# Set-up of a convolution and maxout kernel: where x buffers are zeroed, idle matmuls beside the band, and the engine of some weight differences

## The chip, the cores and the metric

The kernel runs on one core of a Trainium2 chip. The metric is device time in microseconds of one execution. Times inside an execution come from a hardware profile of it, counted from the span's start. The engines are named as in the profile: PE is TensorE (PEld its weight loads), DVE VectorE, ACT ScalarE, POOL GpSimd, SP SyncE, which here only issues transfers (SPq is its queue).

## What is computed

A light convolution over time (7 taps, one softmaxed set of weights for each of 8 heads of 24 channels) is followed by a maxout layer and an output matrix. Shapes: x is 8 x 4160 x 192, so 33280 tokens; w1, w2, w3 are 192 x 768; w_out is 768 x 192.

```python
w = exp(weight - max); w = w / (sum(w) + 1e-09)          # 8 heads x 7 taps
y[b, s, h, g] = sum_k w[h, k] * x_pad[b, s + k, h, g]     # x_pad: 6 rows of zeros ahead
h = maximum(maximum(y @ w1, y @ w2), y @ w3)
out = h @ w_out
```

The kernel uses max(a, b, c) = c + max(0, a - c, b - c): it forms the differences w1 - w3 and w2 - w3 (`wd`), so that ScalarE's Relu gives max(0, a - c), VectorE takes the maximum with b - c, and the part of c goes through one matrix M = w3 @ w_out (`m16`).

## The kernel before

The 33280 tokens make 65 tiles of 512. A tile's stages are: load x as fp32, cast to fp16, convolve as matmuls with a band matrix (`band`, built from the 7 taps of each head), bring the result to channels by tokens, multiply by `wd` (`l1`), and multiply by w_out and M (`st2`). The first four tiles (0 to 3, "dense") are convolved from `xz` straight into channels by tokens; from tile 4 on the convolution's result goes through a DMA transpose (`turn`) and GpSimd makes a second copy of it for the other half of the partitions (`double`).

x buffers and their zeroing. There are seven buffers. Those of blocks 0 to 3 are used again by blocks 7 to 10, in another layout with more rows, some of which must be zero. `get_x` zeroes them on GpSimd when a block asks for its buffer:

```python
def get_x(t):
    if not 0 <= t < NB or t in xin:
        return
    if t < XBUF:                                     # XBUF = 7, NDENSE = 4
        xbuf.append(const.tile([P, NR, D], FP32, name=f"xf_{t}"))
    xf = xbuf[t % XBUF if t < NDENSE + XBUF else NDENSE + (t - NDENSE - XBUF) % 3]
    if NDENSE <= t < NDENSE + XBUF:
        nc.gpsimd.memset(xf[TOK:HALF, 0 if t < XBUF else NQ:NR, :], 0.0)
    xin[t] = [xf, 0, ()]
# load_x(t, eng=nc.sync) calls get_x(t), then issues the loads of the block
```

The beginning: the loads, the idle matmuls that keep TensorE at work, and the band (38 small matmuls into two PSUM tiles, which ScalarE and VectorE copy out):

```python
load_x(0); load_wa(...); load_x(1); load_wb(...); ...      # weights in pieces, then w_out
for t in range(2, 7):
    load_x(t)
...
keep_warm(6, psp, "p")                                     # 6 matmuls of 512 columns, result unused
nc.scalar.activation(out=wexp[:], in_=wk[:], func=AF.Exp, accum_out=wsum[:])
nc.vector.reciprocal(out=wrec[:], in_=wsum[:])
nc.vector.tensor_scalar_mul(out=line[:, 31:31 + KW], in0=wexp[:], scalar1=wrec[:])   # L259
for v in range(2):
    nc.vector.memset(xz[1][v][:], 0.0)
cast_dense(0, (nc.vector.tensor_copy, nc.vector.tensor_copy))                        # L200
CUT = 25
for lo, hi, copy in ((0, CUT, nc.scalar.copy), (CUT, WIN, nc.vector.tensor_copy)):
    for c in range(lo, hi):
        if c % 13 == 0:
            nc.tensor.matmul(beside[:], lhsT=idle[HALF:P, 0:P], rhs=idle[HALF:P, :], ...)  # L269
        nc.tensor.matmul(bps[:, c - lo, :], ...)                                     # L270
    for a in range(4):
        copy(out=band[32 * a:32 * a + 32, ...], in_=bps[:]...)                       # L273
keep_warm(2, psp, "p")
```

The weight differences, and the copies by which one of them reaches the other half of the partitions:

```python
def make_wd(n, j0, j1, eng=nc.vector):                                               # L287
    f = slice(P * j0, P * j1)
    eng.tensor_sub(out=wd[:, n, f], in0=ws[:, n, f], in1=w3s[:, n // 2, f])

def cross_wd():
    nc.vector.tensor_copy(out=wd[0:HALF, NC, :], in_=wd[HALF:P, 0, :])               # L299
    nc.scalar.copy(out=wd[HALF:P, NC, :], in_=wd[0:HALF, 1, :])
```

Where the later tiles meet the queues. In iteration t the loop issues, on the SyncE queue and in this order, the store of tile t - 2, loads, and the transposes of a tile convolved in it; `load_x(9)` comes in iteration 3 ahead of `turn(5)`, which brings tiles 5 and 6:

```python
if t in (3, 4):
    double(t + 1)                                          # GpSimd, L411
...
elif t == 3:
    cast_x(7); cast_x(8)                                   # GpSimd, L183
...
op(lambda t=t: (store(t - 2, 0, 4, (nc.sync,)), load_x(9) if t == 3 else None))
... # l1 and st2 of the iteration, on TensorE; conv(u) and its evictions (L388)
turn(u)                                                    # SyncE, L402
load_on(t)
```

Of the kernel before, what the change touches and what calls it, by code (L numbers as in the profile page):

```python
# [10 lines left out]
FP32 = mybir.dt.float32  # L11
# [4 lines left out]
P = 128  # L16
# [5 lines left out]
NBLK = 512  # L22
# [6 lines left out]
def kernel(  # L29
# [88 lines left out]
# [4 lines that stand above are left out]
        if t < XBUF:  # L122
            xbuf.append(const.tile([P, NR, D], FP32, name=f"xf_{t}"))
        xf = xbuf[t % XBUF if t < NDENSE + XBUF else NDENSE + (t - NDENSE - XBUF) % 3]
        if NDENSE <= t < NDENSE + XBUF:
            nc.gpsimd.memset(xf[TOK:HALF, 0 if t < XBUF else NQ:NR, :], 0.0)  # L126
        assert all(v[0] is not xf for v in xin.values())
        xin[t] = [xf, 0, ()]

    def load_x(t, eng=nc.sync):  # L130
        if not 0 <= t < NB:
            return
        loaded.add(t)
        get_x(t)
        xf = xin[t][0]
        if t < NDENSE:
            todo = [(0, c[3], c[1] * SEQ + c[2], i) for i, c in enumerate(chunks_of[t])]
        else:
            todo = [(HALF * (i // NR) + (0 if s else LAP), KR if s else TOK,
                     b * SEQ + s - (LAP if s else 0), i % NR) for i, (b, s) in enumerate(rows_of(t))]  # L140
        parts = []
        i, n = 0, len(todo)
        row = [c[2] for c in todo]
        while i < n:
            k = i
            while k + 1 < n and todo[k + 1][:2] == todo[i][:2] and row[k + 1] - row[k] == row[i + 1] - row[i]:
                k += 1
            step = row[i + 1] - row[i] if k > i else 0
            p0, rlen, _, q0 = todo[i]
            q1 = todo[k][3] + 1  # L150
            src = bass.AP(tensor=x.tensor, offset=row[i] * D,
                          ap=[[D, rlen], [step * D, q1 - q0], [1, D]])
            eng.dma_start(out=xf[p0:p0 + rlen, q0:q1, :], in_=src)
            if parts and parts[-1][0] == rlen:
                parts[-1] = (rlen, parts[-1][1], q1)
            else:
                parts.append((rlen, q0, q1))
            i = k + 1
        xin[t] = [xf, todo[0][0], parts]
# [31 lines left out]
    def cast_dense(t, copies):  # L191
        xf, _, parts = xin.pop(t)
        for v, copy in enumerate(copies):
            if copy is None:
                continue
            for s in range(CYC // 32):
                cut = GRP * (32 * s // GRP + 1)
                a, b = (32 * s, cut) if v == 0 else (cut, 32 * s + 32)
                for (rl, q0, q1) in parts:
                    copy(  # L200
                        out=xz[t][v][0:rl, q0:q1, :].rearrange("p q (k c) -> p q k c", c=CYC)[:, :, :, a:b],
                        in_=xf[0:rl, q0:q1, :].rearrange("p q (k c) -> p q k c", c=CYC)[:, :, :, a:b])
# [27 lines left out]
    make_identity(nc, ident[:])  # L230
    ident16 = const.tile([P, P], FP16)
    nc.gpsimd.tensor_copy(out=ident16[:], in_=ident[:])
    for t in range(2, 7):
        load_x(t)
    idle = const.tile([P, NBLK], FP16)
    nc.vector.memset(idle[:], 0.0)
    def keep_warm(n, pool=psw, tag="w"):

        ps = pool.tile([P, NBLK], FP32, tag=tag, name="idle")
        for _ in range(n):  # L240
            nc.tensor.matmul(ps[:], lhsT=idle[:, 0:P], rhs=idle[:], start=True, stop=True)  # L241
# [8 lines left out]
        nc.vector.memset(xz[0][v][:], 0.0)  # L250
    band = const.tile([P, NHEAD, BAND_W], FP16)
    nc.vector.memset(band[:], 0.0)
    keep_warm(6, psp, "p")
    wexp = const.tile([NHEAD, KW], FP32)
    wsum = const.tile([NHEAD, 1], FP32)
    nc.scalar.activation(out=wexp[:], in_=wk[:], func=AF.Exp, accum_out=wsum[:])  # L256
# [3 lines left out]
    for v in range(2):  # L260
        nc.vector.memset(xz[1][v][:], 0.0)
    cast_dense(0, (nc.vector.tensor_copy, nc.vector.tensor_copy))
    CUT = 25
    beside = psw.tile([P, NBLK], FP32, tag="w", name="beside")
    for lo, hi, copy in ((0, CUT, nc.scalar.copy), (CUT, WIN, nc.vector.tensor_copy)):
        bps = psq.tile([32, hi - lo, NHEAD], FP32, tag="q", name=f"band_{lo}")
        for c in range(lo, hi):
            if c % 13 == 0:
                nc.tensor.matmul(beside[:], lhsT=idle[HALF:P, 0:P], rhs=idle[HALF:P, :], start=True, stop=True)  # L269
            nc.tensor.matmul(bps[:, c - lo, :], lhsT=line[:, WIN - 1 - c:WIN + 31 - c],  # L270
                             rhs=ident16[0:NHEAD, 0:NHEAD], start=True, stop=True)
        for a in range(4):
            copy(out=band[32 * a:32 * a + 32, :, 32 * a + lo:32 * a + hi],  # L273
                 in_=bps[:].rearrange("p c h -> p h c"))
    keep_warm(2, psp, "p")

# [6 lines left out]
# [3 lines that stand above are left out]
# [5 lines left out]
    def cast_w3(j0, j1):  # L293
        f = slice(P * j0, P * j1)
        nc.gpsimd.tensor_copy(out=w3h[:, 0, f], in_=w3s[:, 0, f])
        nc.gpsimd.tensor_copy(out=w3h[0:HALF, 1, f], in_=w3s[0:HALF, 1, f])

    def cross_wd():
        nc.vector.tensor_copy(out=wd[0:HALF, NC, :], in_=wd[HALF:P, 0, :])  # L299
        nc.scalar.copy(out=wd[HALF:P, NC, :], in_=wd[0:HALF, 1, :])  # L300

    def side(i, c):
# [8 lines left out]
    def transpose_w3(g):  # L311
        ps = psw.tile([P, 2, D], FP32, tag="w", name=f"pt{g}")
        for k in range(2):
            js = slice(P * (2 * g + k), P * (2 * g + k + 1))
            for n in range(2):
                row = slice(0, HALF if n else P)
                nc.tensor.matmul(ps[:, k, P * n:min(P * (n + 1), D)], lhsT=w3h[row, n, js],  # L317
                                 rhs=ident16[row, row], start=True, stop=True)
        nc.scalar.copy(out=w3t[:, 2 * g:2 * g + 2, :], in_=ps[:])
# [39 lines left out]
    def conv_dense(t, copies):  # L359


        yd = dense[t] = ydp.tile([P, NC, NBLK], FP16, tag="yd", name=f"yd_{t}")
        for n, slots_ in enumerate(((0, 1, 2, 3), (4, 5, 4, 5))):
            ps = psw.tile([P, NBLK], FP32, tag="w", name=f"D{n}_{t}")
            for (q, b, row_lo, rlen, lo, hi, cc) in chunks_of[t]:
                for v in range(2):
                    for g, s in enumerate(slots_):
                        h = (32 * s + 31 * v) // GRP
                        nc.tensor.matmul(  # L369
                            ps[32 * g:32 * g + 32, lo:hi],  # L370
                            lhsT=xz[t][v][0:rlen, q, 32 * s:32 * s + 32],
                            rhs=band[0:rlen, h, cc:cc + hi - lo],
                            start=(v == 0), stop=(v == 1), tile_position=(0, 32 * g))
            copies[n](out=yd[:, 2 * n, :], in_=ps[:])  # L374
# [128 lines left out]
    def l1_dense(tiles):  # L503

        meet()
        ps = {}
        for t, j, pools in tiles:
            for i, (pool, tag) in enumerate(pools):
                ps[t, j, i] = pool.tile([P, NBLK], FP32, tag=tag, name=f"l{tag}{i}_{t}_{j}")
                nc.tensor.matmul(ps[t, j, i][:], lhsT=wd[:, i, P * j:P * (j + 1)], rhs=dense[t][:, 0, :],  # L510
                                 start=True, stop=False)
        for t, j, _ in tiles:
            for i in range(2):
                nc.tensor.matmul(ps[t, j, i][:], lhsT=w_of(i, NC - 1, j), rhs=y_all(t, i, NC - 1),  # L514
                                 start=False, stop=True)
        return [lambda t=t, j=j: top(t, j, (ps[t, j, 0], ps[t, j, 1])) for t, j, _ in tiles]
# [95 lines left out]
    make_wd(2, 0, 2)  # L612
    cast_dense(1, (nc.gpsimd.tensor_copy, ACT))
    a, b = l1_dense([(0, 0, PQ), (0, 1, PQ)])
    a()
    cast_w3(0, 2)
    conv_dense(1, (ACT, ACT))
    make_wd(0, 2, 4)
    make_wd(1, 2, 4)
    b()  # L620
    copy_w3(ACT, 2, 6)
# [2 lines left out]
    a()  # L624
    b()
    transpose_w3(0)
    make_wd(0, 4, 6)
    a, b = l1_dense([(0, 2, PQ), (0, 3, WW)])
    cast_w3(2, 6)
    a()  # L630
    make_wd(1, 4, 6)
    b()
    for f in l1_dense([(1, 2, PQ), (1, 3, WW)]):
        f()
    for f in l1_dense([(0, 4, PQ), (0, 5, WW)]):
        f()
    transpose_w3(1)
    transpose_w3(2)
    nc.gpsimd.tensor_copy(out=wo[:], in_=wos[:])
    cast_dense(2, (nc.gpsimd.tensor_copy, nc.gpsimd.tensor_copy))  # L640
    cast_dense(3, (nc.gpsimd.tensor_copy, nc.gpsimd.tensor_copy))
    cast_x(4)
    for f in l1_dense([(1, 4, PQ), (1, 5, WW)]):
        f()
    make_m(0)
    make_m(1)
    st2(0, (10, 10))
    meet()
    conv_dense(2, (ACT, DVE))
    cross_wd()  # L650
    cross(2)
    for u in range(2, NJ):
        st2(0, (5 * u + 5, 5 * u + 5))
# [104 lines left out]
```

## Time and profile before

| | |
|---|---|
| time, median of 3 runs | 461.1 us (460.49 to 464.15) |
| span of the profiled execution | 461.4 us |
| TensorE busy | 453.4 us, 98% |
| VectorE, ScalarE, GpSimd busy | 78%, 69%, 44% |
| idle matmuls L241, first 62 us | 9, 4.4 us busy |
| "beside" matmuls L269 | 3, 1.8 us busy |
| zeroing of x, GpSimd L126 | 7, 6.2 us busy |
| subtractions L287, VectorE | 8, 3.9 us busy |

A line of the profile names the line of the kernel (L126), the engine, the operation and the tiles, written tile first. In the timeline a row merges neighbours of one kind; its first two numbers are start and length in us, and the bracket says how long the engine had been idle and what ended that. A wait that is put down to one engine can be of several. PEclk is the share of its full clock that TensorE was granted; in the first 12 us, before its first record, it is shown as full although the matmuls there are slow.

### The profile page before, as it was taken

To read this page: it belongs to the slowest core of one execution; us is meant where nothing else is said; L and a number is where in the kernel's file an instruction comes from. 1 tells how busy PE (TensorE), PEld (TensorE's weight loads), DVE (VectorE), ACT (ScalarE), POOL (GpSimd) and SP (SyncE) were. 2 spreads that over 40 slices of the span, in tenths; PEclk is the share of its full clock that TensorE was granted. 3 is DMA by queue.
4 is the path that set the end of the run, shared out by engine and by line. 5 is a ranking of instruction groups with operands and counts; after the bars stand their busy time and mean duration, and the time that the engine had idled before them with its cause. 6 is when DMAs were issued, how large, how long until landed. Compare 5 with 4: busy or idle time off the path is not lost.

```text
span 461.4 us, 18767 instructions
## 1 busy us (share of the span) xinstructions
PE 453.4 (98%) x7832; PEld 414.2 (90%) x7832; DVE 359.4 (78%) x617; ACT 317.0 (69%) x605; POOL 204.2 (44%) x227
## 2 busy tenths in 40 slices
PE   8999799999999999999999999999999999999997
PEld 4368689999999999999999999999999999999996
DVE  7757667778878788787878888787887878787776
ACT  3757466667767677766766777676777767676664
POOL 5456455165744354434546454533645344504000
PEclk9999989999999999999999999999999999999999
DMA  7946986687794977959596885859686694525223
GB/s 196 214 83 164 180 172 176 181 192 186 185 209 126 168 163 173 187 120 191 138 182 146 168 199 131 178 133 189 161 180 161 144 182 134 132 72 108 68 70 104
DMA packets 127988, 72.04 MB, mean 156 GB/s; under 512 B 52064, under 2 KB 127711, under 8 KB 127903
## 3 DMA queue, kind: packets, MB, share of 16 engines
q1 hardware_dynamic: 127743, 70.75, 69.2%
q8 instruction: 61, 1.00, 1.0%
q14 instruction: 24, 0.20, 0.2%
q10 hardware_dynamic: 160, 0.10, 0.1%
HBM read 33.28 MB, written 25.56 MB: 128 GB/s over the span
## 4 chain that ended last, share of the span: by engine, by line
PE 96%; DVE 1%; issue 1%; DMA 1%; ACT 1%; POOL 0%; ACTq 0%; POOLq 0%; DVEq 0%
PE po L558 36%; PE lq L494 31%; PE lp L494 21%; PE G L350 3%; PE D L369 1%; DMA yp<-ys 1%; PE lw L510 0%; PE lq L510 0%; PE lp L514 0%; PE pt L317 0%; PE lp L510 0%; POOL yp L411 0%; PE idle L241 0%; PE band L270 0%; ACT L256 0%
## 5 line engine op out<-in xcount | busy, mean ns | idle before, releaser
L558 PE MATMUL po<-wo,h 64*128 64x192 f16 x3120 | 337.6, 243 | 0.2 <-DVE yd L374 0.2
L482 DVE TENSOR_TENSOR h<-r,lq 128x512 f16<-128x512 f16 x385 | 264.0, 686 | 92.4 <-ACT r L481 82.5
L481 ACT ACTIVATE r<-lp 128x512 f16<-128x512 f32 x385 | 229.9, 597 | 121.2 <-PE lp L494 106.4
L494 PE MATMUL lp<-yp,wd 64*128 64x512 f16 x1098 | 296.9, 377 | 1.7 <-POOL yp L411 1.7
L494 PE MATMUL lq<-yp,wd 64*128 64x512 f16 x1098 | 296.7, 377 | 0.9 <-POOL yp L411 0.9
L558 PEld LDWEIGHTS <-h 64*128 64x128 f16 x3120 | 246.4, 94 | 8.9 <-issue 5.7
L494 PEld LDWEIGHTS <-wd 64*128 64x128 f16 x2268 | 179.0, 94 | 13.4 <-issue 2.7
L183 POOL CAST x<-xf 103x768 f16<-103x768 f32 x122 | 97.3, 827 | 118.8 <-DMA xf<-in_x_dram 85.9
L558 PE MATMUL po<-m,yp 64*128 64x192 f16 x732 | 143.6, 244 | 0.0
L411 POOL COPY yp<-yp 64x1536 f16<-64x1536 f16 (+1 forms) x62 | 89.6, 1445 | 88.2 <-DMA yp<-ys 48.6
L567 DVE TENSOR_TENSOR o<-a,po 128x384 f32<-128x384 f32 (+1 forms) x132 | 71.4, 542 | 2.5 <-PE po L558 1.3
L558 PEld LDWEIGHTS <-yp 64*128 64x128 f16 x732 | 67.5, 94 | 0.7
L566 ACT COPY a<-po 128x384 f32<-128x384 f32 (+1 forms) x132 | 61.7, 468 | 1.9 <-PE po L558 1.5
L388 ACT CAST ys<-G 128x384 f16<-128x384 f32 x61 | 26.3, 482 | 10.7 <-PE G L350 10.7
L388 DVE CAST ys<-G 128x384 f16<-128x384 f32 x61 | 31.0, 550 | 0.0
L350 PE MATMUL G<-x,band 39*32 39x192 f16 (+2 forms) x1216 | 17.8, 231 | 0.0
L350 PEld LDWEIGHTS <-band 39*32 39x32 f16 x1216 | 11.3, 91 | 4.9 <-issue 4.7
L494 PE MATMUL lq<-yd,wd 64*128 64x512 f16 x36 | 9.9, 376 | 0.3 <-issue 0.3
L494 PE MATMUL lp<-yd,wd 64*128 64x512 f16 x36 | 9.9, 376 | 0.0
L558 PE MATMUL po<-m,yd 64*128 64x192 f16 x48 | 7.5, 243 | 0.0
L369 PEld LDWEIGHTS <-xz 112*32 112x32 f16 x320 | 4.6, 108 | 2.5 <-issue 1.7
L126 POOL MEMSET xf<- 32x576 f32 (+1 forms) x7 | 6.2, 916 | 0.2
(61 smaller groups left out, 86.3 us busy)
## 6 DMA issues: line engine op xcount, KB each, us to landing
xf<-in_x_dram SPq DMA_DIRECT2D x113, 234.0 KB
out_dram<-o SPq DMA_DIRECT2D x62, 384.0 KB
xf<-in_x_dram SPq DMA_DIRECT2D x7, 204.8 KB
xf<-in_x_dram SPq DMA_DIRECT2D x3, 420.0 KB
ws<-in_moe_w_dram SPq DMA_DIRECT2D x8, 128.0 KB
yp<-ys SPq DMA_TRANSPOSE x62
out_dram<-o SPq DMA_DIRECT2D x5, 192.0 KB
wos<-in_moe_w_out_dram SPq DMA_DIRECT2D x1, 576.0 KB
```

What stands on the lines that cost most here:

```text
L126: nc.gpsimd.memset(xf[TOK:HALF, 0 if t < XBUF else NQ:NR, :], 0.0)
L183: nc.gpsimd.tensor_copy(out=x16s[t0][0:K, :, :, u, r, :].rearrange("p h j c -> p j h c"), in_=xf[0:K, 4 * r:4 * r + 4, :].rearrange("p j ( ...
L350: nc.tensor.matmul(G[2 * (k // per) + i][TOK * j:TOK * (j + 1), k % per, :], lhsT=band[row, h, HALF * i + LAP:HALF * i + KR], rhs=x16s[t0] ...
L369: nc.tensor.matmul(ps[32 * g:32 * g + 32, lo:hi], lhsT=xz[t][v][0:rlen, q, 32 * s:32 * s + 32], rhs=band[0:rlen, h, cc:cc + hi - lo], star ...
L388: copy(out=slots[t][:, i % 2, :, :, GRP * h0:GRP * (h0 + per)].rearrange("p u r (h c) -> p h (u r) c", c=GRP), in_=G[i][:].rearrange("p h ...
L411: nc.gpsimd.tensor_copy(out=yp[HALF * i:HALF * (i + 1), 1, :, :, :, :].rearrange("p i u k n -> p (i u k n)"), in_=yp[HALF * (1 - i):HALF * ...
L481: nc.scalar.activation(out=r[:], in_=ps[0][:], func=AF.Relu)
L482: nc.vector.tensor_max(out=hs[t][:, j, :], in0=r[:], in1=ps[1][:])
L494: nc.tensor.matmul(ps[i][:], lhsT=w_of(i, c, j), rhs=y_all(t, i, c), start=(c == 0), stop=(c == NC - 1))
L558: nc.tensor.matmul(ps[b0, i][:, s % 2, :], lhsT=a, rhs=b, start=first, stop=last)
L566: nc.scalar.copy(out=a[:, ss, :], in_=ps[s0, 0][:, ss, :])
L567: nc.vector.tensor_add(out=outs[t][:, s0:s + 1, :], in0=a[:, ss, :], in1=ps[s0, 1][:, ss, :])
```

## The change

Set-up is to be rearranged in four ways. Zeroing leaves `get_x`: a function `zero_x` does it for blocks 4 to 6 after GpSimd's first casts, and for the later rows of the buffers of blocks 0 to 3 after the cast of block 4, so that no load later in the kernel needs a memset first. The idle matmuls inside the band's loop go; one of the idle matmuls ahead of it moves behind it, and ScalarE's share of the band's copies grows from 25 columns to 28. The differences of the last third of w1 and w2 are formed on GpSimd, as is one of the two copies of `cross_wd`, which moves ahead of the cast of block 3. Some other calls of set-up change their order.

```diff
@@ get_x, zero_x
-        if NDENSE <= t < NDENSE + XBUF:
-            nc.gpsimd.memset(xf[TOK:HALF, 0 if t < XBUF else NQ:NR, :], 0.0)
+    def zero_x(t):
+        if t >= NDENSE:
+            get_x(t)
+        xf = xbuf[t]
+        nc.gpsimd.memset(xf[TOK:HALF, 0 if t >= NDENSE else NQ:NR, :], 0.0)
@@ the beginning
-    for t in range(2, 7):
+    for t in range(2, NDENSE):
         load_x(t)
-    keep_warm(6, psp, "p")
+    keep_warm(5, psp, "p")
-    CUT = 25
-    beside = psw.tile([P, NBLK], FP32, tag="w", name="beside")
+    CUT = 28
-            if c % 13 == 0:
-                nc.tensor.matmul(beside[:], lhsT=idle[HALF:P, 0:P], rhs=idle[HALF:P, :], start=True, stop=True)
-    keep_warm(2, psp, "p")
+    keep_warm(3, psp, "p")
@@ cross_wd
-        nc.vector.tensor_copy(out=wd[0:HALF, NC, :], in_=wd[HALF:P, 0, :])
+        nc.gpsimd.tensor_copy(out=wd[0:HALF, NC, :], in_=wd[HALF:P, 0, :])
@@ the order of set-up
     a, b = l1_dense([(0, 0, PQ), (0, 1, PQ)])
+    make_wd(0, 2, 4)
     a()
     cast_w3(0, 2)
+    for t in range(NDENSE, XBUF):
+        zero_x(t)
+        load_x(t)
     conv_dense(1, (ACT, ACT))
-    make_wd(0, 2, 4)
     make_wd(1, 2, 4)
...
     transpose_w3(0)
-    make_wd(0, 4, 6)
-    a, b = l1_dense([(0, 2, PQ), (0, 3, WW)])
+    make_wd(0, 4, 6, nc.gpsimd)
+    make_wd(1, 4, 6, nc.gpsimd)
+    for f in l1_dense([(0, 2, PQ), (0, 3, WW)]):
+        f()
     cast_w3(2, 6)
-    a()
-    make_wd(1, 4, 6)
-    b()
     for f in l1_dense([(1, 2, PQ), (1, 3, WW)]):
         f()
+    nc.gpsimd.tensor_copy(out=wo[:], in_=wos[:])
     for f in l1_dense([(0, 4, PQ), (0, 5, WW)]):
         f()
     transpose_w3(1)
+    cast_dense(2, (nc.gpsimd.tensor_copy, nc.gpsimd.tensor_copy))
+    for f in l1_dense([(1, 4, PQ), (1, 5, WW)]):
+        f()
     transpose_w3(2)
-    nc.gpsimd.tensor_copy(out=wo[:], in_=wos[:])
-    cast_dense(2, (nc.gpsimd.tensor_copy, nc.gpsimd.tensor_copy))
+    cross_wd()
     cast_dense(3, (nc.gpsimd.tensor_copy, nc.gpsimd.tensor_copy))
     cast_x(4)
-    for f in l1_dense([(1, 4, PQ), (1, 5, WW)]):
-        f()
+    for t in range(NDENSE):
+        zero_x(t)
     make_m(0)
     make_m(1)
     st2(0, (10, 10))
     meet()
     conv_dense(2, (ACT, DVE))
-    cross_wd()
     cross(2)
```

## The prediction

> **What bounds the kernel now.** I read the page first, then a table of stages by windows, then the timelines of the SyncE queue, GpSimd and TensorE around the one stage that looked wrong, and last the chain of waits of the first 14 us. The page says that TensorE is busy almost throughout:
>
> ```profile
> PE 453.4 (98%) x7832; PEld 414.2 (90%) x7832; DVE 359.4 (78%) x617; ACT 317.0 (69%) x605; POOL 204.2 (44%) x227
> ...
> PEclk9999989999999999999999999999999999999999
> ```
>
> From about 65 us on two tiles take 12.6 to 14 us (spacing of the L567 rows), and the change touches nothing there. So the gain can only be TensorE time lost or delayed before that. In PEclk one slice of 40 (the sixth, 57.7 to 69.2 us) has a lower digit. The windows (columns: length, then busy us and number of instructions of PE, PEld, DVE, ACT and POOL, granted clock, DMA share, GB/s) find the stage:
>
> ```profile
> 49.00:52.40 3.40, 3.40 (x53) 3.23 (x48) 2.72 (x5) 2.29 (x5) 0.00 (x0) 1.00 1.14 174
> 52.40:55.75 3.35, 0.75 (x10) 0.45 (x7) 1.37 (x3) 0.83 (x2) 2.93 (x2) 1.00 1.13 216
> 55.75:60.00 4.25, 4.25 (x39) 3.54 (x40) 1.38 (x2) 1.40 (x3) 3.14 (x4) 0.60 1.21 162
> 60.00:63.40 3.40, 3.40 (x56) 3.09 (x54) 2.52 (x4) 2.31 (x5) 2.93 (x2) 1.00 0.96 161
> ```
>
> TensorE works 0.75 of 3.35 us, and then runs at a granted clock of 0.60 on the average. Why it stops is in the timelines (start, length, what; in brackets the idle time before). GpSimd, then the SyncE queue:
>
> ```profile
> 41.39 1.59 POOL L183 CAST x<-xf 103x768 f16<-103x768 f32 x2 [1.15 <-PE G L350]
> 42.94 0.25 POOL L180 MEMSET xf<- 7x192 f32 x1
> 44.07 1.60 POOL L183 CAST x<-xf 103x768 f16<-103x768 f32 x2 [0.89 <-DMA xf<-in_x_dram]
> 45.73 1.08 POOL L126 MEMSET xf<- 32x576 f32 x2
> 52.71 2.99 POOL L411 COPY yp<-yp 64x1536 f16<-64x1536 f16 x2 [5.89 <-DMA yp<-ys]
> ```
>
> ```profile
> 38.91 1.21 SPq L597 DMA_DIRECT2D out_dram<-o  x2
> 46.33 0.81 SPq L153 DMA_DIRECT2D xf<-in_x_dram  x2
> 47.23 3.47 SPq L402 DMA_TRANSPOSE yp<-ys  x2
> ```
>
> Nothing leaves the SyncE queue between 40.12 and 46.33. It holds the load of x block 9, which get_x lets wait for the zeroing of its buffer, and that memset stands in GpSimd's order behind the casts of blocks 7 and 8, which wait for their own loads. Behind the load, in the same queue, stand the transposes of tiles 5 and 6, whose input was ready when the two evictions ended, at 42.26 (ACT and DVE rows of L388). They start 5 us late; GpSimd then doubles yp (two copies of 1.47 us, 52.71 to 55.70), and TensorE resumes at 54.23 and 55.75.
>
> The first 14 us hold the second loss. DVE's and TensorE's timelines, and one later row:
>
> ```profile
> 3.19 1.25 DVE L259 TENSOR_SCALAR line<-wexp,wrec 8x7 f16<-8x7 f32 x1
> 4.39 2.22 DVE L200 CAST xz<-xf 112x240 f16<-112x240 f32 x6
> 6.94 1.08 DVE L273 CAST band<-band 32x104 f16<-32x104 f32 x4 [0.34 <-PE band L270]
> 18.63 0.90 DVE L287 TENSOR_TENSOR wd<-ws,w3s 128x256 f16<-128x256 f32 x1
> ```
>
> ```profile
> 4.93 0.60 PE L269 MATMUL beside<-idle 64*128 64x512 f16 x1
> 5.46 0.50 PE L270 MATMUL band<-ident,line 8*32 8x8 f16 x13
> 5.90 0.60 PE L269 MATMUL beside<-idle 64*128 64x512 f16 x1
> 6.43 0.48 PE L270 MATMUL band<-ident,line 8*32 8x8 f16 x12
> ```
>
> 56 numbers take 1.25 us, and of the six casts the first takes 1.51 us, the same shape later 0.27. Both end as one of GpSimd's memsets of 32x1536 ends (1.73 to 5.76, three of 1.37 to 1.39 us).
>
> [...] The trace agrees: the two rows above, and the 0.90 us of a subtraction that otherwise takes 0.42, beside a GpSimd cast from 18.10 to 19.25. [...] The trace agrees: a granted clock of 0.5 for 3.41 us after the stop, and matmuls of 512 columns start every 0.43 us before 12.2 us and every 0.22 after. [...]
>
> **The change part by part.**
> (1) zero_x takes the zeroing of the later rows of blocks 0 to 3 out of get_x, and puts four memsets (4 x 0.57 = 2.3 us) behind the cast of block 4. GpSimd is idle there: 26.95 to 31.16. The load of block 9 then has nothing to wait for, and the transposes go out when the evictions end, 5 us earlier. The loss: the second addition of each tile (row L567) starts at 46.36, 54.93, 64.39, 71.69 and 77.97, so the two disturbed tiles take 18.03 us where the next two take 13.58: 4.45 us. By parts: gaps in TensorE's starts of 1.8 and 1.2 us, 3.0 together, and half of 3.41 us at half clock, 1.7. [...]in a median run I count 3.0 + 0.7 x 1.7 = 4.2.
> (2) The three memsets of blocks 4 to 6 (4.1 us) leave 1.73 to 5.76. The scaling of the band's line then takes some 0.15 us like the reciprocal before it: the band can start at about 3.4 in place of 4.5, and that is where five idle matmuls (1.20 + 5 x 0.43) end, hence 6 to 5. Without the two "beside" matmuls in its middle (2 x 0.54 = 1.08; the first filled a wait) the band takes 0.50 + 0.43 + 0.41 = 1.3 us and ends at 4.7. VectorE's casts of x block 0 can't start before 4.3 (the semaphore counts put its second half there) and need 1.1 us without the block: 5.4 in place of 6.61. Then four band copies, of 10 columns in place of 13 (1.08 to about 1.0): 6.4. ScalarE's four, of 28 columns, end by 5.9. So the first convolution starts at about 6.35 in place of 7.80: 1.45 us.
> (3) Two subtractions go to GpSimd, behind the three memsets[...]. In the chain the wait at 18.06 to 19.58 for one of them cost a group of 8 matmuls 2.0 us in place of 1.5: 0.5 us.
> (4) cross_wd's half, 0.36 us of VectorE, moves to GpSimd at about 21 us; TensorE doesn't wait for it: nothing.
> Against this: weights and blocks 1 to 3 arrive by a DMA that is full (share 1.04 to 1.11 at 5 to 9 us), not sooner than now; block 1 at 8.39, the last weights at 13.67, w_out at 18.05. The shifted uses stand behind these, with little to spare. [...] I take 0.2 off for these: set-up 1.95 - 0.2 = 1.75 us.
> Sum: 4.2 + 1.75 = 5.95, less 0.35 for the first rival: 5.6 us.
>
> **The rivals.**
> A: the transposes take the place of the memset as the wait. The loads of blocks 7, 8 and the stores before them keep the DMA engines full until 45.9; load 9 (479 KB, at some 220 GB/s 2.2 us) now comes right behind, so the transposes land at about 49.5 by the present clock, not 2.4 us after issue as those of tile 4 on an empty queue. Doubling then ends at 51.0 and 52.5, and TensorE wants it at 52.3 to 52.6. A rest of 0 to 1.5 us may stay; I count 0.35. If the transposes were as slow as now, only 1 us of (1) would come: 458.
> B: set-up is bound by transfers, and (2) and (3) only lengthen later waits. For it: the full DMA. Against it: from 9.6 to 29 us TensorE is idle under 1 us. It would give 457.
> C: TensorE's clock. [...]up to 1.7 us back, 457. In this profile the clock rose only at 12.2, beside matmuls or not, which speaks against it.
> D: blocked VectorE at 10 to 16 us delays h, and l1 waits for its PSUM: 1 us back.
>
> **Range and chances.** 461.1 - 5.6 = 455.5. The three runs before spread by 3.7 us[...], so a median can lie 1.5 to the side; A to D take up to 3, all of (1) and (2) in full without deductions gives 453.7. 8 in 10: 452.0 to 458.5. Two per cent faster is 451.9, below the sum of everything that I can find: 0.07. Slower by 2% would need a new stall of 9 us on top: 0.01.
>
> **What would show it.** SyncE's queue issues load 9 at about 38 to 39 us and the transposes of tile 5 right behind the evictions; no L126 row on GpSimd after 30 us; PEclk without its dip and windows of 3.4 us with full TensorE from 48 to 60. L259 near 0.15 us, the first L200 cast near 0.3 us, the first convolution at 6.2 to 6.6 us. L287 on GpSimd at 0.6 to 0.9 us, and no wait of l1 for it. I am wrong if TensorE still waits for L411 by more than 1 us, if the first l1 after tile 1 starts less than 1 us earlier than 28.93, or if the lost time turns up as waits for DMA of x or w_out.

## The result and the profile after

| | before | after |
|---|---|---|
| time, median (range) of 4 runs each | 462.22 us (460.49 to 464.15) | 457.13 us (456.25 to 457.55) |
| ratio, 95% interval | | 0.9886 (0.9838 to 0.9935) |
| span of the profiled execution | 461.4 us | 454.5 us |

The change takes 5.1 us off, 1.1%; the interval allows 3.0 to 7.5 us. Two later comparisons gave 0.9903 (0.9869 to 0.9937) and 0.9889 (0.9853 to 0.9925). The two profiled executions differ by more, 6.9 us; below it will matter that one profile is one draw.

The page of the changed kernel, its row of busy engines. It has no PEclk row, as no change of the clock was recorded in this execution:

```profile
PE 449.2 (99%) x7829; PEld 413.3 (91%) x7829; DVE 357.4 (79%) x614; ACT 317.0 (70%) x605; POOL 206.8 (46%) x230
```

Three matmuls fewer (the "beside" ones), and three VectorE instructions that went to GpSimd. TensorE's idle time fell from 8.0 us of 461.4 to 5.3 of 454.5. The windows around the place where it used to stop (columns as before: length, busy us and number of PE, PEld, DVE, ACT, POOL, clock, DMA share, GB/s):

```profile
45.00:48.40 3.40, 3.40 (x108) 3.01 (x104) 2.46 (x6) 2.57 (x6) 1.01 (x1) 1.00 1.00 197
48.40:51.75 3.35, 3.35 (x53) 3.24 (x50) 2.77 (x6) 2.35 (x5) 3.23 (x4) 1.00 1.19 209
51.75:56.00 4.25, 4.25 (x67) 4.11 (x64) 3.22 (x7) 2.76 (x5) 2.78 (x4) 1.00 1.02 222
```

TensorE is full in all three, where before one window held 0.75 us of matmuls and the next ran at 0.60. The clock column says 1.00 here only because nothing was recorded; that the clock was full is seen in the matmuls of 512 columns of `lp`, which start every 0.22 us within their groups from 45 to 62 us, and every 0.43 us in the window of half clock before. The reason stands in the timelines, GpSimd's and then the SyncE queue's:

```profile
27.95 2.13 POOL L133 MEMSET xf<- 32x576 f32 x4
...
47.39 2.99 POOL L413 COPY yp<-yp 64x1536 f16<-64x1536 f16 x2 [4.40 <-DMA yp<-ys]
```

```profile
39.41 0.96 SPq L158 DMA_DIRECT2D xf<-in_x_dram  x2
40.46 3.71 SPq L404 DMA_TRANSPOSE yp<-ys  x2
```

The four memsets lie in GpSimd's idle time, the load of block 9 leaves at 39.41 in place of 46.33, the transposes at 40.46 in place of 47.23, and the doubling starts at 47.39 in place of 52.71. The two disturbed tiles, by the ends of the second addition (44.48 and 58.09, in place of 46.90 and 64.93), take 13.61 us in place of 18.03: 4.42 less.

Set-up, VectorE's timeline and then TensorE's:

```profile
3.19 0.22 DVE L264 TENSOR_SCALAR line<-wexp,wrec 8x7 f16<-8x7 f32 x1
...
4.37 1.00 DVE L205 CAST xz<-xf 112x240 f16<-112x240 f32 x6
5.29 0.97 DVE L275 CAST band<-band 32x80 f16<-32x80 f32 x4
```

```profile
3.47 1.17 PE L272 MATMUL band<-ident,line 8*32 8x8 f16 x38
...
6.05 1.91 PE L371 MATMUL D<-band,xz 112*32 112x103 f16 x80
...
10.17 0.39 PE L516 MATMUL lp<-yd,wd 64*128 64x512 f16 x1 [0.24 <-DVE wd L289]
...
22.15 0.34 PE L328 MATMUL pm<-wo,w3t 128*128 128x192 f16 x2 [0.30 <-ACT w3t L321]
```

The scaling of the line takes 0.22 us in place of 1.25, six casts 1.00 in place of 2.22, and the first convolution starts at 6.05 in place of 7.80. The last two rows are new waits: for a weight difference, and for a transposed w3 that M is made from. What the first hangs on is in the chain of waits of the first 12 us (start, length, what):

```profile
3.63 5.37 DMA w3s<-in_moe_w_dram
...
9.02 0.64 DVE w3s L293
...
9.69 0.43 DVE wd L289
```

A piece of w3 lands at 9.0; two VectorE instructions later TensorE goes on. In this execution it is no longer the start of set-up that sets this point, but a transfer.

### The profile page after: what moved, and what is told of

It reads as the page before. It is cut to its first block, busy times and chain, and to the rows that moved or that the text cites. A ratio compares the mean times of both kernels' runs of the same rounds, so it can differ in the third digit from the quotient of the medians.

```text
span 454.5 us, 18761 instructions
## 1 busy us (share of the span) xinstructions
PE 449.2 (99%) x7829; PEld 413.3 (91%) x7829; DVE 357.4 (79%) x614; ACT 317.0 (70%) x605; POOL 206.8 (46%) x230
## 4 chain that ended last, share of the span: by engine, by line
PE 96%; DMA 1%; SPq 1%; DVE 0%; ACT 0%; issue 0%; DVEq 0%
PE po L560 36%; PE lq L496 31%; PE lp L496 22%; PE G L352 3%; DMA w3s<-in_moe_w_dram 1%; PE D L371 1%; PE lw L512 1%; PE lp L516 0%; PE lp L512 0%; SPq L217 0%; SPq L158 0%; PE pt L319 0%; PE lq L512 0%; PE lw L516 0%; DVE yd L376 0%
## 5 line engine op out<-in xcount | busy, mean ns | idle before, releaser
L390 ACT CAST ys<-G 128x384 f16<-128x384 f32 x61 | 26.3, 482 | 10.2 <-PE G L352 10.2
L205 POOL CAST xz<-xf 112x240 f16<-112x240 f32 (+2 forms) x15 | 4.2, 322 | 8.6 <-DVE yd L376 7.2
```

What stands on the lines that cost most here:

```text
L390: copy(out=slots[t][:, i % 2, :, :, GRP * h0:GRP * (h0 + per)].rearrange("p u r (h c) -> p h (u r) c", c=GRP), in_=G[i][:].rearrange("p h ...
```

## The experiments

Each ratio is against the kernel before on the same chip. My theory was the sum of the prediction: most of the gain comes from the SyncE queue (part 1), a smaller one from set-up. The rivals were its A (the transposes stay a wait of their own) and B (set-up is bound by transfers).

**The zeroing put back, all else changed (e1_late_zero).** The memsets of blocks 7 to 10 are in get_x again:

```diff
 (get_x of the changed kernel)
+        if XBUF <= t < NDENSE + XBUF:
+            nc.gpsimd.memset(xf[TOK:HALF, NQ:NR, :], 0.0)
 (set-up)
-    for t in range(NDENSE):
-        zero_x(t)
```

> The changed kernel, with the zeroing of the buffers of blocks 7 to 10 put back to where each block asks for its buffer; all else as changed. Theory (the memset ahead of load 9 holds the transposes of tiles 5 and 6 in SyncE's queue): TensorE stops again for about 3 us near 50 us, the granted clock dips for 3.4 us or not[...], and the kernel is 3 to 4.7 us slower than the changed one, 460 to 461.5 us, 1 to 2 us faster than before. Rival (the earlier set-up alone gives the transposes the room they lacked): no stop, within 1 us of the changed kernel, 457.

Measured: 462.1 us, ratio 0.9971 (0.9946 to 0.9997). Against the change's 0.9886 to 0.9903 this is 3.1 to 3.9 us lost, each with some 2 us of doubt either way, and 1.3 us (0.1 to 2.5) are what the rest of the change is worth alone. The stop is back. SyncE queue, then TensorE, of this run:

```profile
43.91 0.81 SPq L160 DMA_DIRECT2D xf<-in_x_dram  x2
44.81 2.55 SPq L406 DMA_TRANSPOSE yp<-ys  x2
```

```profile
53.04 0.37 PE L498 MATMUL lp<-yp,wd 64*128 64x512 f16 x1 [2.04 <-POOL yp L415]
...
54.56 0.37 PE L498 MATMUL lq<-yp,wd 64*128 64x512 f16 x1 [0.93 <-POOL yp L415]
```

GpSimd's row of that time merges two memsets of 0.54 us, for blocks 9 and 10, from 43.32 to 44.40. The load of block 9 leaves as the first ends, the transposes follow the load, and TensorE waits 2.04 and 0.93 us for the doubling. Half clock did not follow here; the last section sets this stop beside those that it followed.

**The zeroing left late, the load taken out of the way (e2_load_behind).** In the kernel before, the load of block 9 is no longer issued ahead of the transposes but by load_on behind them. The memset stays where it was:

```diff
-            op(lambda t=t: (store(t - 2, 0, 4, (nc.sync,)), load_x(9) if t == 3 else None))
+            op(lambda t=t: store(t - 2, 0, 4, (nc.sync,)))
```

> The kernel before, with nothing changed but the order of two things on SyncE's queue: the load of block 9 is issued behind the transposes of tiles 5 and 6 and not ahead of them; the memsets stay late. Theory (order in the queue, not GpSimd's time): the transposes leave at about 42.3 us, the stop at 52 us is gone, 3 to 4.5 us faster than before, about 457.5 to 458.5. Rival 1 (GpSimd's time for the late memsets is what delays the doubling): no gain, 461 to 462. Rival 2 (the late load of block 9 becomes the next wait): a new TensorE stop later on, gain under 2 us.

Measured: 460.1 us, ratio 0.9934 (0.9914 to 0.9955), so 3.1 us. The SyncE queue:

```profile
42.48 3.35 SPq L402 DMA_TRANSPOSE yp<-ys  x2
45.96 1.87 SPq L153 DMA_DIRECT2D xf<-in_x_dram  x4
```

The transposes go at 42.48, though the memset still comes only at 45.36, and TensorE no longer waits for the doubling. (What is left there is one gap of 0.64 us at 54.24, put down to VectorE; whether the later load has a part in it isn't shown.) So it was not GpSimd's time for the memset that TensorE waited for, but the load that waits for it, in one queue ahead of the transposes.

**Only the early zeroing (e5_zero_only).** The kernel before, with the four memsets behind cast_x(4) and get_x zeroing only the buffers of blocks 4 to 6:

```diff
-        if NDENSE <= t < NDENSE + XBUF:
-            nc.gpsimd.memset(xf[TOK:HALF, 0 if t < XBUF else NQ:NR, :], 0.0)
+        if NDENSE <= t < XBUF:
+            nc.gpsimd.memset(xf[TOK:HALF, 0:NR, :], 0.0)
 (set-up, behind cast_x(4))
+    for t in range(NDENSE):
+        nc.gpsimd.memset(xbuf[t][TOK:HALF, NQ:NR, :], 0.0)
```

> The kernel before with only the zeroing of the buffers of blocks 7 to 10 moved, to behind the cast of block 4 (part 1 of the change alone). Theory: load 9 leaves at about 40 us and the transposes behind it at about 42.3; no TensorE stop near 52 us, no clock dip; 3 to 4.5 us faster than before, ratio 0.990 to 0.9935, a little better than with the load issued behind the transposes, since block 9 also comes earlier. Rival A (load 9 now directly ahead of the transposes makes them land late): a stop of 0.5 to 1.5 us stays, ratio 0.994 to 0.997.

Measured: 459.34 us, ratio 0.9910 (0.9880 to 0.9940): 4.2 us, with an interval of 2.8 to 5.6. The SyncE queue:

```profile
40.80 1.97 SPq L153 DMA_DIRECT2D xf<-in_x_dram  x2
42.86 3.55 SPq L402 DMA_TRANSPOSE yp<-ys  x2
```

TensorE is busy 3.35 of 3.35 us from 48.40 to 51.75, and doesn't wait for the doubling. By the medians part (1) alone carries some four fifths of the change.

**Two halves of the band's part, each alone (e3_no_beside, e4_memsets_moved).** The first takes out only the three "beside" matmuls:

```diff
-            if c % 13 == 0:
-                nc.tensor.matmul(beside[:], lhsT=idle[HALF:P, 0:P], rhs=idle[HALF:P, :], start=True, stop=True)
```

> The kernel before without the three idle matmuls among those of the band, nothing else. Theory (VectorE's casts, held up by a GpSimd memset until 5.9 us, set the first convolution as soon as the band ends sooner): the band ends at 5.8 in place of 6.9, but the first convolution starts only 0.3 to 0.4 us earlier, at about 7.45, and the time is 0 to 0.5 us less. Rival (the idle matmuls lie on the path alone): the first convolution starts 1.1 us earlier, at 6.7.[...]

The second moves only the memsets and loads of blocks 4 to 6 behind cast_w3(0, 2):

```diff
-    for t in range(2, 7):
+    for t in range(2, NDENSE):
         load_x(t)
 (behind cast_w3(0, 2))
+    for t in range(NDENSE, XBUF):
+        load_x(t)
```

> The kernel before with only the zeroing and loads of blocks 4 to 6 moved behind GpSimd's first casts; idle matmuls, subtractions and late zeroing stay. Theory: the scaling of the line drops from 1.25 to about 0.2 us and the first cast of x from 1.5 to 0.3, but the band still begins behind seven idle matmuls at about 4.4 us and ends at 6.8; the first convolution starts at about 7.65 in place of 7.80: 0 to 0.3 us gained. So neither this nor the removal of the idle matmuls alone gives the 1.75 us of the changed kernel. Rival (the held-up VectorE is the path alone): first convolution at 6.7, 1 us gained.

Measured: 463.28 us, 1.0007 (0.9980 to 1.0033), and 463.91 us, 1.0009 (0.9990 to 1.0028). Neither is worth anything that these intervals show. The profile of e3_no_beside, VectorE and then TensorE:

```profile
4.78 1.82 DVE L200 CAST xz<-xf 112x240 f16<-112x240 f32 x6 [0.35 <-DMA xf<-in_x_dram]
6.52 1.08 DVE L270 CAST band<-band 32x104 f16<-32x104 f32 x4
```

```profile
4.49 1.17 PE L267 MATMUL band<-ident,line 8*32 8x8 f16 x38 [0.54 <-DVE xz L261]
...
7.37 1.91 PE L366 MATMUL D<-band,xz 112*32 112x103 f16 x80 [0.74 <-DVE band L270]
```

The band ends at 5.66, 1.25 us sooner, but the first convolution starts only 0.43 sooner: VectorE's six casts, beside GpSimd's memsets (1.72 to 5.75 in this run), take 1.82 us where they take 1.00 in the profile after; they end at 6.6, and the copies of the band come after that. In e4_memsets_moved the casts are quick (1.01 us, and the scaling of the line 0.22) but the band, with the idle matmuls in it, ends at 6.13, and the convolution starts at 7.01. That is sooner than expected, but in this execution the clock was full from 3.99 to 7.40 us, and idle matmuls that take 0.60 us elsewhere took 0.39 to 0.42. In each run the half that was left in place still holds the start.

**Both halves together (e6_band_part).** e3 and e4 in one, with the change's 5 and 3 idle matmuls and CUT of 28, all else as before.

```diff
-    keep_warm(6, psp, "p")
+    keep_warm(5, psp, "p")
-    CUT = 25
+    CUT = 28
-    keep_warm(2, psp, "p")
+    keep_warm(3, psp, "p")
```

> The kernel before with both parts of the band's stretch together: zeroing and loads of blocks 4 to 6 moved behind GpSimd's first casts, no idle matmuls in the band, 5 and 3 idle matmuls around it, 28 columns for ScalarE; subtractions and late zeroing as before. Theory: the two only pay together; the first convolution starts at 6.0 to 6.4 in place of 7.8, the first l1 of tile 2 about 1.3 us earlier, ratio 0.996 to 0.998, where each alone gave 1.0007 and 1.0009. Rival B (set-up is bound by transfers): the first convolution is earlier, but later waits for weights or x take it back, ratio 0.999 to 1.001.

Measured: 462.75 us, 0.9983 (0.9961 to 1.0006), 0.8 us with an interval from 1.8 to -0.3. TensorE:

```profile
6.33 1.90 PE L366 MATMUL D<-band,xz 112*32 112x103 f16 x80 [0.32 <-DVE band L270]
...
10.78 0.39 PE L511 MATMUL lp<-yd,wd 64*128 64x512 f16 x1 [1.36 <-DVE wd L284]
```

The convolution starts at 6.33, almost to the hundredth what the prediction worked out (6.35); then 1.36 us of the gain stand as a wait for the third weight difference. Rival B holds for this point.

**The subtractions back on VectorE (e7_wd_on_dve, and again as r_wd_on_dve).**

```diff
-    make_wd(0, 4, 6, nc.gpsimd)
-    make_wd(1, 4, 6, nc.gpsimd)
+    make_wd(0, 4, 6)
+    make_wd(1, 4, 6)
```

> The changed kernel with the two moved subtractions back on VectorE, in their new place in the order. Theory (part 3 brought its 0.5 us by leaving VectorE): 0.3 to 0.6 us slower than the changed kernel. Rival (the 0.90 us subtraction of before only met GpSimd's cast of w_out; with the new order and the memsets gone from there it takes 0.42 us again): within 0.2 us of the changed kernel.

> The kernel with the two subtractions back on VectorE once more, beside the changed kernel on the same chip: the first look had 0.9863 against 0.9903, intervals that overlap. Theory (the engine of these two doesn't matter once the memsets are out of the way): equal within 0.4 us. Rival (GpSimd's subtractions cost a microsecond): 1 us faster again.

Measured: 456.72 us, 0.9863 (0.9835 to 0.9892), and 457.48 us, 0.9885 (0.9853 to 0.9917). In the same two comparisons the changed kernel itself got these (expectations first):

> The changed kernel itself again, beside the others on one chip, to have the sum to which the parts are held: ratio 0.988 to 0.991. If the parts add up (late zeroing 0.9925, set-up 0.997), 0.9895; if they hide each other it is nearer to the larger alone.

> The changed kernel once more, as the measure for the other three: ratio 0.988 to 0.991.

Measured: 458.06 us, 0.9903 (0.9869 to 0.9937), and 458.11 us, 0.9889 (0.9853 to 0.9925). The intervals overlap, with the medians 1.3 and 0.6 us in favour of VectorE, where the theory of the first had 0.3 to 0.6 us the other way: moving the subtractions to GpSimd bought nothing that these runs show. The second repeat shows rival A at work, on TensorE:

```profile
51.22 0.37 PE L496 MATMUL lp<-yp,wd 64*128 64x512 f16 x1 [1.07 <-POOL yp L413]
...
52.74 0.37 PE L496 MATMUL lq<-yp,wd 64*128 64x512 f16 x1 [0.93 <-POOL yp L413]
```

The code is that of the profile after, which has no such wait. Here the transposes left at 40.78 (after: 40.46), but by the trace's semaphore counts the second landed at 49.60, not at 47.28.

**The wait for the weights taken away (e8_wb_first).** In the changed kernel the second piece of weights is loaded ahead of x block 1:

```diff
-    load_x(1)
 (behind load_wb(slice(0, PW)))
+    load_x(1)
```

> The changed kernel with one order of loads changed: the first pieces of the lower rows of the weights (which the third subtraction needs, and TensorE's first matmuls of 64 rows) go out ahead of x block 1. Theory (rival B in part: after the change set-up is bound by the arrival of these rows): they land some 1.5 us earlier, TensorE's wait for the third subtraction near 10 us (0.24, 0.8, 1.6, 1.7 us in four runs) goes, x block 1 lands about 0.7 us later and its convolution starts at 10.6 to 11.0; 0.2 to 0.8 us faster than the changed kernel. Rival (the arrival of x block 1 binds just as much): the wait only moves to that convolution, 0 +- 0.3 us.

Measured: 457.78 us, 0.9888 (0.9852 to 0.9925), the same as the change. The wait is gone (the rows land at 6.1 to 6.8, the second convolution starts at 10.58, and l1 of tile 2 at 26.91, the earliest of all), yet TensorE stops for the doubling again:

```profile
51.61 0.37 PE L496 MATMUL lp<-yp,wd 64*128 64x512 f16 x1 [2.00 <-POOL yp L413]
...
53.13 0.37 PE L496 MATMUL lq<-yp,wd 64*128 64x512 f16 x1 [0.93 <-POOL yp L413]
```

The transposes landed at 49.98 there. TensorE arrived sooner at a transfer that didn't come sooner, and waited longer: 2.00 us against 1.07 in the second repeat of the change.

**All that had seemed good (e9_best).** e7 and e8 together, and transpose_w3(2) moved ahead of the last l1 group, against the new wait for w3t:

```diff
+    transpose_w3(2)
     for f in l1_dense([(1, 4, PQ), (1, 5, WW)]):
         f()
-    transpose_w3(2)
```

> A version meant to beat both: the changed kernel, the two subtractions back on VectorE, the order of loads of the run before, and the last transposes of w3 ahead of the last pair of dense matmuls, so that their copy no longer holds the product w3 @ w_out up by 0.30 us. Theory: 0.5 to 1 us faster than the changed kernel, ratio 0.986 to 0.988. Rival (x block 2, which lands at 20 to 22 us, and its casts bind from there): no more than the run with the subtractions back on VectorE alone.

Measured: 457.68 us, 0.9883 (0.9851 to 0.9915). Not better than the change. The wait at M is gone, but other gaps between starts came: 0.62 us in l1 at 17.1, 0.58 ahead of st2 at 23.5, and 1.26 at 51.3 for the doubling. No version that ran beats the change by more than the intervals.

## Why the prediction was near, point by point

**Part (1) less rival A, the SyncE queue: mechanism and size right.** A run can measure only both together, for which 4.2 - 0.35 = 3.85 us were predicted. e5_zero_only has 4.2 with this part alone, e1_late_zero shows 3.1 to 3.9 lost without it, and the profiled pair, in which nothing of A is left, has 4.42. e2_load_behind shows the mechanism by itself: same late memset, and the transposes not behind it. One size inside it was too large: the 3.0 us of the stop are whole distances between starts, of which TensorE was idle for 2.60 (1.66 and 0.94), and the tiles' 4.45 less 1.7 for the half clock leave 2.75. The chance of 0.7 for the half clock, an estimate of the author's, was fair: it followed the full stop in 4 of 5 profiles (before, e3, e4, e6; not e1).

**Part (2), the band: right at the start, then partly given back to B.** The predicted start of the first convolution was 6.35, 1.45 us sooner. How the gain fared on TensorE, in means of three profiles with the old set-up (before, e2, e5) and six with the new one (after, its two repeats, e1, e7 and its repeat):

| starts of | old | new | gain |
|---|---|---|---|
| first convolution | 7.80 | 6.16 | 1.64 |
| second convolution | 12.43 | 11.02 | 1.41 |
| third convolution | 25.40 | 24.32 | 1.08 |
| l1 of tile 2 | 28.48 | 27.39 | 1.09 |

Between the first and the second convolution lies the wait for the third difference (0.24 us in the profile after, 0.82 and 0.54 in repeats; e5, with the old set-up, had 0.55): its rows land at 9.0 to 10.1 us, though set-up starts sooner. The prediction had looked at block 1, the last weights and w_out under B, but not at this piece.

The clock is in this table too. It became full at 12.2, 12.6 and 9.6 us in the three old profiles, and at 8.4 to 10.2 in the five new ones that recorded it. Where it did so at the same time, 9.57 us in e5 and in the first repeat of the change, the starts of l1 of tile 2 are 27.86 and 27.67, only 0.19 apart. Whether the new set-up brings the full clock sooner or these executions only happened to differ so, these few profiles can't tell; the 1.1 us are the gain with the clock's part in it.

**Part (3): the term that failed.** 0.5 us were to come from two subtractions on GpSimd; the table shows 0.33 lost in the stretch that holds them. From second to third convolution the old order takes 12.80 to 12.84 us in four profiles (e2, e4, e5, e6), and 13.28 and 13.39 in two (before, e3), the ones in which TensorE waited for the subtraction. So the wait that was read off one profile isn't there in most executions. The new order takes 13.26 to 13.33 in six of its profiles and 13.40 in the repeat of e7, with a new gap of 0.55 us between starts at M, which waits for ScalarE's w3t (the row at 22.15): before, an l1 group lay between transpose_w3(2) and make_m, now none does. With the subtractions on VectorE (13.33 and 13.40) it is no shorter than on GpSimd (13.26): the engine is not what mattered. The step that failed is this one: the prediction wrote down the removed wait, +0.5, and no new one, where the stretch got 0.33 longer. Part (4) was set at nothing, and no wait for cross_wd shows in the profile after.

**The sum.** Set-up was to bring 1.75 us and brings about 1.1 by the table. The profiled pair alone shows 1.90 (28.93 to 27.03), which flatters the prediction: the clock rose at 12.2 us in that execution before, at 9.6 in e5 with the same set-up.

**Rival A, deducted with 0.35: rather too little.** Its mechanism is as stated: the load, 479 KB, goes right ahead of the transposes, and when those land varies (47.28 in the profile after, 49.60 in the second repeat, 49.98 in e8). By TensorE's idle time ahead of the doubled tiles, of the eight profiles with early zeroing four have no such rest (after, the first repeat, e5 and e7), and four have 0.43 (the repeat of e7), 0.93 (e9), 2.00 (the second repeat) and 2.93 us (e8). The mean is 0.8, in the middle of the 0 to 1.5 that the prediction gave, with two profiles beyond it. In none of them did half clock follow the wait.

**Rivals C and D: no sign.** In the new set-up the clock was full from a time between 7.9 and 10.2 us on, not later than with the old one (9.6 to 12.6 in before, e2 and e5; the profile after has no record of it). In e5 it became full at 9.57, after 3.41 us in which TensorE ran part of the band, idle matmuls and the first convolution. Beside GpSimd's three memsets (10.99 to 15.00 in the profile after) VectorE's subtraction of 128x256 at 11.83 took 0.42 us, as it does without them, and VectorE's rows at 10 to 16 us led to no wait of l1. The 0.2 us of "Against this" were the author's estimate.

In all 5.6 us were predicted and 5.1 measured. The terms as measured, 3.1 to 4.2 for (1) less A and 1.1 for set-up, make 4.2 to 5.3. So the term that was mis-sized is set-up, 1.75 for about 1.1, by a missed wait for weights and by the 0.5 of part (3). The other two experiments on set-up agree with a small term: 1.3 us in e1_late_zero and 0.8 in e6_band_part, though the interval of the second includes nothing at all. That the sum came within 0.5 us says less than it seems to, as the measured gain has an interval of 3.0 to 7.5. The rest of the distance from 455.5 to 457.13 is the base: the three runs before had a median of 461.1, and 462.22 with the fourth. Not tried: the early zeroing with the load of block 9 also behind the transposes, as in e2, which would show whether A's rest can be had.

## What to carry to other kernels

Where a queue issues in order (here SyncE's: the transposes left at 47.23 us behind the load of 46.33, and at 42.48 where that load stood behind them), look for a transfer that waits for another engine, and ask what stands behind it: that, not the transfer, is what the wait cost here, and moving either out of the way was enough (3.1 and 4.2 us). When two things hold one start (here idle matmuls on TensorE, and memsets beside which VectorE's scaling and first cast took 1.25 and 1.51 us in place of 0.22 and 0.28), taking out one moves it by only a part: 0.43 and 0.79 us each alone, 1.47 together. Take them out together, and then find the next thing that lands on time only by a little; here what was left of it was 0.8 us of time, with an interval that includes nothing. A wait of half a microsecond in one profile may be missing in the next execution (that for the subtraction showed in two profiles of six); look for it in a second profile before it goes into a sum.

## What was not expected of the hardware

**TensorE stops that no instruction explains.** In several runs TensorE stopped at one of a few places, the same in the program's count of matmuls each time (most often ahead of the 480th and the 608th), for a time that differs from run to run. At the one near 30 us, in the first convolution of tile 3, TensorE's timeline in e4_memsets_moved has this row:

```profile
31.81 0.96 PE L369 MATMUL D<-band,xz 112*32 112x103 f16 x35 [2.63 <-issue]
```

The stop there is 1.63 us in e5, 0.69 in e2 and 0.37 before, and the profile after has none. "issue" says that nothing in the profile was waited for. In four cases (before, e2, e4, and the first repeat of the change, there at 52.3 us) a packet of 16384 bytes of the queue named "instruction" ends 1.3 to 1.5 us before TensorE goes on (in e4 it runs from 28.94 to 30.41). The two places lie 128 matmuls apart. Packet and stop go together in these four cases, but that the packet is the cause is a guess that no run tested; in the profile after two such packets end at 30.58 and 34.37, and TensorE makes no stop of over 0.2 us after either. In e4 half clock for 6.83 us followed this stop, and the tile it fell in took 14.05 us against 9.49 in the profile before.

**The clock in steps.** The recorded stretches of one clock are whole multiples of 3.41 us, up to the last record: 44.37 in before (13 of them), 20.48 and 6.83 in e4 (6 and 2). The steps of 3.41 us, counted on from the first record, can be laid over TensorE's idle time. The steps that half clock followed held 1.99 us of idle time in before, 2.80 in e3, 2.12 and 2.17 in e4 and 2.19 in e6. In e1 the 2.97 us of waiting fell into two steps with 1.78 and 1.20 us idle, in e8 the 2.93 into two with 1.28 and 1.65, and no half clock followed. No other whole step at full clock from 12 us on, in any profile with a record, breaks this order. So in these profiles 2.0 us idle of 3.41 were followed by half clock and 1.8 were not, and stops of much the same length (2.60 us in before, 2.97 in e1) were followed by it or not according to how they lay on the steps.

**GpSimd's subtraction** took 0.73 us for 128x256 (two of them from 15.09 to 16.50 in the profile after), 1.7 times VectorE's 0.42. No run had shown it before the change: the range of 0.6 to 0.9 us that the prediction looked for was an estimate of the author's.
